# Attention and gated MLP on one core: loads of batch 1 taken ahead of w_out, transposes spread over the h steps, and k of batch 0 loaded as fp32 and cast on chip

## The chip, the cores and the metric

One NeuronCore of a Trainium2 chip runs the whole program. The metric is device time in microseconds (us) of one execution. PE is TensorE, the matmul engine; the profile calls GpSimd POOL, and SPq, ACTq and POOLq are the queues in which SyncE, ScalarE and GpSimd issue transfers. The granted clock is the share of its full clock that PE got, as the profile records it. An execution is called slow when it is over 1.5% above the fastest of the same kernel; ratios below use fast runs only.

## The reference

```python
# q, k, v: (8, 8, 576, 64) = batch, heads, sequence, head_dim; p: (8, 8, 32, 64)
p_packed = sm_attn(p, k, v)               # 32 rows attend to 576
out = sm_attn(q, p_packed, p_packed)      # 576 rows attend to the 32
x = out.transpose(0, 2, 1, 3).reshape(8 * 576, 512)
h = x @ w_in                              # 512 -> 2048
result = (h * cos(h)) @ w_out             # 2048 -> 512, fp32
```

`sm_attn` is softmax(scale · q kᵀ) v. All inputs are fp32 in HBM; the kernel works in bf16.

## The kernel before

The program is one hand-made schedule: instructions of an engine run in the order in which they are written. For each batch b there is an attention part that ends in `a2n[b]` (the normalised second softmax) and `PPW[b]` (the packed p times w_in), then an *h phase* of 16 steps. One step is four matmuls, a cosine on ScalarE (ACT) and a multiplication on VectorE (DVE) that writes `gT`. The output matmuls of batch b, gT times w_out, are *filler*: 64 or 80 matmuls of 0.2155 us that are slipped in wherever PE would otherwise wait during batch b+1. Batch 0 has no filler beside it. The k, q and v inputs are cast to bf16 in their transfers by GpSimd's queue; k and q are then transposed on PE in the first batches and by a DMA transpose on SyncE (`xbar`) later. In the code below `pe_T` transposes on PE, `s1` and `s2` are the scores and exponentials of the two softmaxes, `a1_pe` transposes the first one's result, `pp` multiplies it by v, `ppw` multiplies that by a quarter of w_in, `pack_p` transposes p, and `warm(n)` issues n matmuls on zeros that only keep PE busy.

```python
def load(n, b):                       # cast load, fp32 -> bf16, GpSimd's queue; one buffer for each of k, q, v
    bf[n, b] = bf_pool.tile([TP, H, C * D], BF16, name=n + "bf", tag=n + "bf")
    G.dma_start(out=bf[n, b], in_=srcs[n][b].rearrange("h (p c) d -> p h (c d)", c=C))

def xbar(n, b):                       # DMA transpose, SyncE's queue
    t = xT[n, b] = att_pool.tile([128, H * 3, TP], BF16, name=n + "T", tag=n + "T")
    nc.sync.dma_start_transpose(out=t, in_=bf[n, b].rearrange("p h x -> p (h x)"))
# ... (cut)
nc.sync.dma_start(out=p_raw[:, 0:2, :], in_=p_rows[:, 0:2, :])
load("k", 0); load("v", 0); make_identity(nc, ident); load("q", 0)
load_w_in(0); load_w_in(1)
G.dma_start(out=p_raw[:, 2:, :], in_=p_rows[:, 2:, :])
load_w_in(2); load_w_in(3)
for n in range(4): load_w_out(n)
load("k", 1); load("v", 1); load("q", 1); load("k", 2); load("v", 2); load("q", 2)
# ...
warm(7); dup_p(0, 2); pack_p(0, 1)    # p of batches 0 and 1: cast on DVE, transposes on PE
warm(9); pe_T("k", 0, (V, ACT, V)); s1(0); permute_v(0, V)
# ... attention of batch 0
for fc in range(NFC):                 # h phase of batch 0
    h_mm(0, fc)()
    if fc in (1, 4, 7): ppw(0, 1 + fc // 3)
    if fc == 10: pack_p(1, 3)
set_filler(0)
# ... attention of batch 1, with k2's transposes and s1(2) in it, 43 fillers
def begin_loads(b):                   # loads of batch 3 wait for the transpose of k3
    G.tensor_copy(out=gate, in_=xT["k", b][0:1, 0, 0:1])
    for n, i in (("v", b), ("q", b), ("k", b + 1)): load(n, i)
permute_v(2); xbar("q", 2); xbar("k", 3)     # DMA transposes BEFORE the h phase of batch 1
slot(1, [...], [(8, lambda: begin_loads(3)), (12, lambda: pw2(2))])
for s in range(2, B): ...             # batches 2 to 7
```

The softmax here doesn't subtract the row's maximum and nothing guards it: scores larger than these inputs give would overflow.

## Time and profile before

| | value |
|---|---|
| time, 3 runs | 263.75, 263.75, 261.2 us |
| span of the profiled run | 261.1 us, mean granted clock 0.993 |
| first h matmul of batch 0 | 20.27 us |
| last gT of batch 0 | 37.2 us |
| first h matmul of batch 1 | 58.27 us |
| last gT of batch 1 | 77.8 us |
| start of batch 3's second scores | 106.04 us |

The last five rows are landmarks from the timeline; they cut the program into stretches. The prediction shows the rows of the page and reads them. Two lines of the timeline of the kernel before: the cast of p (the number in brackets is DVE's wait for it) and the transposes of k of batch 0, which start when its cast load has landed.

```profile
2.89 0.40 DVE L303 CAST p_bf<-p_raw 128x128 bf16<-128x128 f32 x2 [0.64 <-DMA p_raw<-in_p_dram]
...
7.81 1.19 PE L101 MATMUL psA<-ident,kbf 96*128 96x96 bf16 x24 [0.88 <-DMA kbf<-in_k_dram]
```

### The profile page before, as it was taken

What the parts mean: (1) busy time and instruction counts of PE and PEld (TensorE: products, weight loads), DVE (VectorE), ACT (ScalarE), POOL (GpSimd) and SP (SyncE); (2) the same over time, 40 slices, a digit from 0 to 9 for tenths busy, and PEclk for the clock granted to TensorE, in tenths of its full rate; (3) what the DMA queues carried; (4) which work ended last, traced back from release to release, by engine and by line L of the source; (5) the groups of instructions that cost most, each with busy time, mean ns of one, the idle gap of its engine ahead of it and who ended that gap; (6) DMA issues with size and microseconds to landing.
All of it is one profiled execution on the core that took longest, in us unless ns stands there. A gap on an engine that the chain in (4) does not pass through costs nothing.

```text
span 261.1 us, 5031 instructions
## 1 busy us (share of the span) xinstructions
PE 236.6 (91%) x2004; PEld 133.3 (51%) x2037; DVE 165.6 (63%) x253; ACT 166.6 (64%) x270; POOL 53.6 (21%) x67
## 2 busy tenths in 40 slices
PE   8675759898989999999999999999989999999993
PEld 3443425644644565456545654465446564565452
DVE  2448864839875677658875676578846775687110
ACT  1378762297687766886788666877786576884000
POOL 8523002250404040504050304020310000000000
PEclk9999997999999999999999999999999999999999
DMA  6999999999499989599939994989294111111232
GB/s 90 203 227 208 206 204 179 180 177 197 77 191 209 198 134 231 108 191 164 220 81 191 171 219 103 158 179 173 77 139 109 40 43 40 40 46 47 69 83 80
DMA packets 62919, 37.09 MB, mean 142 GB/s; under 512 B 35520, under 2 KB 58304, under 8 KB 62896
## 3 DMA queue, kind: packets, MB, share of 16 engines
q0 software_dynamic: 23168, 18.81, 47.8%
q1 hardware_dynamic: 39568, 17.83, 32.7%
q8 instruction: 16, 0.26, 0.4%
q10 hardware_dynamic: 160, 0.13, 0.2%
q14 instruction: 7, 0.06, 0.1%
HBM read 37.22 MB, written 9.44 MB: 179 GB/s over the span
## 4 chain that ended last, share of the span: by engine, by line
PE 72%; DMA 13%; ACT 6%; DVE 4%; issue 2%; POOL 1%; DVEq 0%; POOLq 0%; ACTq 0%
PE ot L270 42%; PE psA L220 20%; DMA kbf<-in_k_dram 7%; DMA w_in_bf<-in_moe_w_in_dram 6%; PE psA L181 3%; PE psA L162 2%; DVE gT L227 2%; PE psA L101 1%; PE ot L259 1%; ACT cosT L224 1%; PE psA L197 1%; PE psA L123 1%; ACT a2u L189 1%; ACT L430 1%; ACT PPW L74 1%
## 5 line engine op out<-in xcount | busy, mean ns | idle before, releaser
L270 PE MATMUL ot<-w_out_bf,gT 128*128 128x512 bf16 x481 | 125.2, 381 | 1.7 <-issue 1.0
L227 DVE TENSOR_TENSOR gT<-psA,cosT 128x576 bf16<-128x576 f32 x128 | 93.8, 754 | 28.7 <-ACT cosT L224 27.2
L224 ACT ACTIVATE cosT<-psA 128x576 bf16<-128x576 f32 x128 | 81.5, 651 | 30.3 <-PE psA L220 28.2
L220 PE MATMUL psA<-a2n,PPW 128*128 128x288 bf16 x512 | 81.2, 285 | 7.4 <-DVE gT L227 3.6
L270 PEld LDWEIGHTS <-gT 128*128 128x128 bf16 x512 | 48.0, 98 | 44.9 <-issue 7.8
L220 PEld LDWEIGHTS <-PPW 128*128 128x128 bf16 x512 | 49.9, 97 | 39.9 <-issue 12.5
L76 DVE CAST PPW<-psA 128x1024 bf16<-128x1024 f32 x22 | 26.9, 1221 | 11.8 <-PE psA L181 11.8
L231 POOL COPY joint<-gT 128x512 bf16<-128x512 bf16 x16 | 9.7, 612 | 102.2 <-DVE gT L227 102.2
L76 DVE COPY osb<-ot 128x512 f32<-128x512 f32 (+1 forms) x19 | 12.8, 672 | 17.6 <-PE ot L270 14.1
L207 DVE SCALAR_TENSOR_TENSOR a2n<-a2u,r,lns 128x576 bf16<-128x576 bf16 x16 | 12.4, 814 | 16.0 <-ACT lns L205 16.0
L74 ACT COPY osb<-ot 128x512 f32<-128x512 f32 (+1 forms) x18 | 10.4, 575 | 17.9 <-PE ot L270 13.2
L76 POOL COPY vp<-vbf 96x3072 bf16<-96x3072 bf16 x6 | 16.5, 2747 | 0.6 <-DMA vbf<-in_v_dram 0.6
L132 ACT ACTIVATE a<-psA 128x576 bf16<-128x576 f32 x16 | 10.2, 648 | 8.3 <-PE psA L123 8.3
L199 ACT ACTIVATE lns<-psA 128x576 f32<-128x576 f32 x16 | 10.4, 653 | 5.7 <-PE psA L197 5.2
L74 ACT CAST PPW<-psA 128x1024 bf16<-128x1024 f32 x10 | 10.1, 1012 | 5.5 <-PE psA L181 5.5
L181 PE MATMUL psA<-w_in_bf,ppT 64*32 64x512 bf16 x256 | 11.9, 382 | 1.3 <-DVE gT L227 0.9
L189 ACT ACTIVATE a2u<-psA,rs 128x576 bf16<-128x576 f32 x16 | 11.0, 736 | 2.6 <-PE psA L123 2.4
L270 PE MATMUL ot<-w_out_bf,joint 128*128 128x512 bf16 x48 | 12.3, 379 | 0.2
L172 ACT CAST ppT<-psA 64x128 bf16<-64x128 f32 x16 | 4.2, 260 | 11.2 <-PE psA L101 6.4
L83 POOL DMA_DIRECT2D kbf<-in_k_dram x8 | 6.3, 786 | 22.1 <-PE psA L101 18.0
L444 POOL COPY gate<-a1T 1x1 bf16<-1x1 bf16 x5 | 0.9, 180 | 46.2 <-DMA a1T<-a 46.2
L224 ACT ACT_TABLE_LOAD x8 | 10.3, 1283 | 0.1
(54 smaller groups left out, 150.8 us busy)
## 6 DMA issues: line engine op xcount, KB each, us to landing
kbf<-in_k_dram POOLq DMA_DIRECT2D x8, 576.0 KB, 11.4
vbf<-in_v_dram POOLq DMA_DIRECT2D x8, 576.0 KB, 6.6
qbf<-in_q_dram POOLq DMA_DIRECT2D x8, 576.0 KB, 9.4
out_dram<-osb SPq DMA_DIRECT2D x24, 192.0 KB, 2.9
out_dram<-osb SPq DMA_DIRECT2D x22, 128.0 KB, 2.4
w_in_bf<-in_moe_w_in_dram POOLq DMA_DIRECT2D x4, 512.0 KB, 15.9
w_out_bf<-in_moe_w_out_dram POOLq DMA_DIRECT2D x4, 512.0 KB, 20.2
out_dram<-osb SPq DMA_DIRECT2D x26, 64.0 KB, 2.1
```

The source lines that it names most:

```text
L74: ACT.copy(out=out, in_=in_)
L76: eng.tensor_copy(out=out, in_=in_)
L132: ACT.activation(out=a1[b % 2][:, y, :, 0:TP].rearrange("p (e m) x -> p e m x", e=2), in_=ps[y][:, :, 0:HS].rearrange("p e (m x) -> p e m ...
L181: nc.tensor.matmul(ps[32 * x:32 * x + 32, y, :], ppT[b % 2][r, 2 * x + y, :], w_in_bf[r, x, n * 512:(n + 1) * 512], start=True, stop=True)
L189: ACT.activation(out=a2u[b][:, y].rearrange("p (e x) -> p e x", e=2), in_=ps[y][:, :, 0:HS], func=AF.Exp, scale=rs1[b][:, y:y + 1])
L199: ACT.activation(out=lns[b][:, y].rearrange("p (e x) -> p e x", e=2), in_=ps[:, :, 0:HS], func=AF.Ln)
L207: V.scalar_tensor_tensor(out=a2n[b][:, y], in0=a2u[b][:, y], scalar=r1[b][:, y:y + 1], in1=lns[b][:, y], op0=ALU.mult, op1=ALU.mult)
L220: nc.tensor.matmul(ps[:, e, 0:HS], PPW[b][:, y, fc * 128:(fc + 1) * 128], a2n[b][:, y, e * HS:(e + 1) * HS], start=(y == 0), stop=(y == 1))
L224: ACT.activation(out=csv, in_=ps[:, :, 0:HS], func=AF.Sin, bias=PI_HALF)
L227: V.tensor_tensor(out=gT[b][:, fc, :].rearrange("p (e x) -> p e x", e=2), in0=ps[:, :, 0:HS], in1=csv, op=ALU.mult)
L231: G.tensor_copy(out=joint[b // 2][:, fc - 7:fc + 1, j0:j0 + 64], in_=gT[b][:, fc - 7:fc + 1, 512:576])
L270: nc.tensor.matmul(ps, w, w_out_bf[:, fc, :], start=(fc == 0), stop=(fc == NFC - 1))
```

## The change

The intent has three parts. **Head:** k0 comes as plain fp32 in two halves by SyncE's queue and is cast by DVE and ACT, so the cast queue starts with v0; v0's permutation is split over DVE and GpSimd; p moves to ScalarE's queue. **Order of loads:** k1, v1 and q1 come ahead of w_out, so PE need not wait for k1 at 35 to 39 us. **Pacing:** k1 is transposed inside batch 0's h phase, k2 and q2 inside batch 1's, and filler is spread evenly. For this k gets two bf16 and two transposed buffers. The cut parts of the diff also compute the first two output chunks of batch 0 side by side, cast the rest of p on GpSimd instead of DVE and re-pace the filler of later batches.

```diff
-    nc.sync.dma_start(out=p_raw[:, 0:2, :], in_=p_rows[:, 0:2, :])
-    load("k", 0)
+    k0 = first.tile([TP, H, C * D], FP32, name="k0")
+    for hh in (slice(0, 4), slice(4, 8)):
+        nc.sync.dma_start(out=k0[:, hh], in_=k[0, hh].rearrange("h (p c) d -> p h (c d)", c=C))
+    nc.scalar.dma_start(out=p_raw[:, 0:2, :], in_=p_rows[:, 0:2, :])
     load("v", 0)
     make_identity(nc, ident)
     load("q", 0)
-    (w_in 0, 1, p, w_in 2, 3, w_out 0..3, k1, v1, q1, k2, v2, q2)
+    (w_in 0..3, p, k1; later in program order v1, q1, w_out 0..3, k2, v2)
 ... (cut)
-    pe_T("k", 0, (V, ACT, V))
+    for a in (0, 4):
+        copy(V, bf["k", 0][:, a:a + 3], k0[:, a:a + 3])
+        copy(ACT, bf["k", 0][:, a + 3:a + 4], k0[:, a + 3:a + 4])
+        if a == 0:
+            warm(2)
+            pe_T("k", 0, (V, ACT, V), (0,))
+            warm(5)
+    pe_T("k", 0, (V, ACT, V), (1, 2))
     s1(0)
-    permute_v(0, V)
+    permute_v(0, V, G)
 ... (cut; in batch 0's h phase:)
-            ppw(0, 1 + fc // 3)
+            ppw(0, 1 + fc // 3, ACT)
+        if fc == 12:
+            pe_T("k", 1)
 ... (cut; batch 1, and its h phase:)
-    permute_v(2); xbar("q", 2); xbar("k", 3)
-    slot(1, [...], [(8, lambda: begin_loads(3)), (12, lambda: pw2(2))])
+    slot(1, [(1, tk("k", 2, 0)), (2, tk("k", 2, 1)), (3, tk("k", 2, 2)), (4, lambda: ppw(1, 3, ACT)),
+             (6, lambda: pack_p(3, B)),
+             (8, tk("q", 2, 0)), (9, tk("q", 2, 1)), (10, tk("q", 2, 2)), (10, lambda: load("q", 3)),
+             (10, lambda: load("k", 4)), (11, lambda: xbar("k", 3))], 4)
 ... (cut: s1(2), attention of batch 2 and s1(3) now follow batch 1's h phase)
```

More of the change, by code (lines that the diff above doesn't have):

```diff
@@ L39 @@
     const = ctx.enter_context(tc.tile_pool(name="const", bufs=1))
+    first = ctx.enter_context(tc.tile_pool(name="first", bufs=1))
     bf_pool = ctx.enter_context(tc.tile_pool(name="bf", bufs=1))
@@ L81, in load, with permute_v, pe_T @@
     def load(n, b):
-        bf[n, b] = bf_pool.tile([TP, H, C * D], BF16, name=n + "bf", tag=n + "bf")
+        bf[n, b] = bf_pool.tile([TP, H, C * D], BF16, name=n + "bf", tag=n + "bf", bufs=2 if n == "k" else 1)
         G.dma_start(out=bf[n, b], in_=srcs[n][b].rearrange("h (p c) d -> p h (c d)", c=C))
-    def permute_v(b, eng=G):
+    def permute_v(b, eng=G, split=None):
         vp[b] = vp_pool.tile([TP, C, H * D], BF16, name="vp", tag="vp")
-        copy(eng, vp[b].rearrange("p c (h d) -> p c h d", h=H),
-             bf["v", b].rearrange("p h (c d) -> p c h d", c=C))
+        dst = vp[b].rearrange("p c (h d) -> p c h d", h=H)
+        src = bf["v", b].rearrange("p h (c d) -> p c h d", c=C)
+        if split is None:
+            copy(eng, dst, src)
+        else:
+            copy(eng, dst[:, :, 0:4], src[:, :, 0:4])
+            copy(split, dst[:, :, 4:8], src[:, :, 4:8])
     def xbar(n, b):
-        t = xT[n, b] = att_pool.tile([128, H * 3, TP], BF16, name=n + "T", tag=n + "T")
+        t = xT[n, b] = att_pool.tile([128, H * 3, TP], BF16, name=n + "T", tag=n + "T", bufs=2 if n == "k" else 1)
         nc.sync.dma_start_transpose(out=t, in_=bf[n, b].rearrange("p h x -> p (h x)"))
-    def pe_T(n, b, engs=(V, V, V)):
-        t = xT[n, b] = att_pool.tile([128, H * 3, TP], BF16, name=n + "T", tag=n + "T")
+    def pe_T(n, b, engs=(V, V, V), groups=(0, 1, 2)):
+        if 0 in groups:
+            xT[n, b] = att_pool.tile([128, H * 3, TP], BF16, name=n + "T", tag=n + "T", bufs=2 if n == "k" else 1)
+        t = xT[n, b]
         flat = bf[n, b].rearrange("p h x -> p (h x)")
-        for i in range(3):
+        for i in groups:
             ps = psa(BF16)
@@ L147, in a1_xbar, with a1_pe @@
                                     in_=a1[b % 2].rearrange("p a c x -> p (a c x)"))
-    def a1_pe(b):
-        t = a1T[b] = att_pool.tile([128, 2, C, 128], BF16, name="a1T", tag="a1T")
-        for y in range(2):
+    def a1_pe(b, ys=(0, 1)):
+        if 0 in ys:
+            a1T[b] = att_pool.tile([128, 2, C, 128], BF16, name="a1T", tag="a1T")
+        t = a1T[b]
+        for y in ys:
             ps = psa(BF16)
@@ L265, in out_gen @@
     def out_gen(b):
-        for c in range(n_chunks(b)):
-            ps = O.tile([128, DM], FP32, name="ot", tag="ot")
-            for fc in range(NFC):
-                w = joint[b // 2][:, fc, :] if c == 4 else gT[b][:, fc, c * 128:(c + 1) * 128]
-                nc.tensor.matmul(ps, w, w_out_bf[:, fc, :], start=(fc == 0), stop=(fc == NFC - 1))
-                if fc < NFC - 1:
-                    yield
-            osb = o_pool.tile([128, DM], FP32, name="osb")
-            copy((V, ACT)[n_out[0] % 2], osb, ps)
-            n_out[0] += 1
-            for a, z, rows in pieces_of(b, c):
-                nc.sync.dma_start(out=rows, in_=osb[a:z, :])
-            yield
+        groups = [(0, 1), (2,), (3,)] if b == 0 else [(c,) for c in range(n_chunks(b))]
+        for grp in groups:
+            pss = {c: O.tile([128, DM], FP32, name="ot", tag="ot") for c in grp}
+            for f0 in range(0, NFC, 4):
+                for c in grp:
+                    for fc in range(f0, f0 + 4):
+                        w = joint[b // 2][:, fc, :] if c == 4 else gT[b][:, fc, c * 128:(c + 1) * 128]
+                        nc.tensor.matmul(pss[c], w, w_out_bf[:, fc, :],
+                                         start=(fc == 0), stop=(fc == NFC - 1))
+                        if fc == NFC - 1:
+                            osb = o_pool.tile([128, DM], FP32, name="osb")
+                            copy((V, ACT)[n_out[0] % 2], osb, pss[c])
+                            n_out[0] += 1
+                            for a, z, rows in pieces_of(b, c):
+                                nc.sync.dma_start(out=rows, in_=osb[a:z, :])
+                        yield
     filler = [None, 0]
@@ L299, in load_w_out, with dup_p @@
                     in_=moe_w_out.rearrange("(a p) n -> p a n", p=128)[:, n * 4:(n + 1) * 4, :])
-    def dup_p(a, b):
+    def dup_p(a, b, eng):
         for t in range(2):
-            V.tensor_copy(out=p_bf[:, a:b, t, :], in_=p_raw[:, a:b, :])
+            eng.tensor_copy(out=p_bf[:, a:b, t, :], in_=p_raw[:, a:b, :])
     def warm(n):
@@ L307, in warm @@
             nc.tensor.matmul(wps, wz[:, 0:128], wz, start=True, stop=True)
-    nc.sync.dma_start(out=p_raw[:, 0:2, :], in_=p_rows[:, 0:2, :])
-    load("k", 0)
+    k0 = first.tile([TP, H, C * D], FP32, name="k0")
+    for hh in (slice(0, 4), slice(4, 8)):
+        nc.sync.dma_start(out=k0[:, hh], in_=k[0, hh].rearrange("h (p c) d -> p h (c d)", c=C))
+    nc.scalar.dma_start(out=p_raw[:, 0:2, :], in_=p_rows[:, 0:2, :])
+    bf["k", 0] = bf_pool.tile([TP, H, C * D], BF16, name="kbf", tag="kbf", bufs=2)
     load("v", 0)
@@ L313 @@
     load("q", 0)
-    load_w_in(0)
-    load_w_in(1)
+    for n in range(4):
+        load_w_in(n)
     G.dma_start(out=p_raw[:, 2:, :], in_=p_rows[:, 2:, :])
-    load_w_in(2)
-    load_w_in(3)
-    for n in range(4):
-        load_w_out(n)
     load("k", 1)
-    load("v", 1)
-    load("q", 1)
-    load("k", 2)
-    load("v", 2)
-    load("q", 2)
     wz = const.tile([128, 512], BF16, name="wz")
@@ L337 @@
     warm(7)
-    dup_p(0, 2)
+    dup_p(0, 2, V)
     pack_p(0, 1)
-    warm(9)
-    pe_T("k", 0, (V, ACT, V))
+    for a in (0, 4):
[6 more added lines that the diff above has]
+    pe_T("k", 0, (V, ACT, V), (1, 2))
     s1(0)
-    permute_v(0, V)
+    permute_v(0, V, G)
+    load("v", 1)
     warm(3)
@@ L348 @@
     pe_T("q", 0, (V, ACT, V))
+    load("q", 1)
+    for n in range(4):
+        load_w_out(n)
+    dup_p(2, 16, G)
+    load("k", 2)
+    permute_v(1, G)
+    load("v", 2)
     s2(0)
@@ L354 @@
     warm(6)
-    dup_p(2, 16)
     for fc in range(NFC):
@@ L358, with slot, pw2, tk @@
         if fc in (1, 4, 7):
-            ppw(0, 1 + fc // 3)
+            ppw(0, 1 + fc // 3, ACT)
         if fc == 10:
             pack_p(1, 3)
+        if fc == 12:
+            pe_T("k", 1)
+    def slot(s, hooks, keep=0, heavy={}):
+        left = filler[1] - keep
+        weight = [1 + heavy.get(fc, 0) for fc in range(NFC)]
+        for fc in range(NFC):
+            h_mm(s, fc)()
+            quota = (left * sum(weight[:fc + 1])) // sum(weight) - (left + keep - filler[1])
+            first = quota
+            while hooks and hooks[0][0] == fc:
+                if first == quota and fc in heavy:
+                    first = quota // 2
+                    fill(first)
+                hooks.pop(0)[1]()
+            fill(quota - first if first != quota else quota)
+    def pw2(b, n=0):
+        ppw(b, n)
+        ppw(b, n + 1)
+    def tk(n, b, i):
+        return lambda: pe_T(n, b, (V, V, V), (i,))
     set_filler(0)
     ACT.preload_act_table_set(EXP_SET)
-    fill(4)
-    pe_T("k", 1)
-    fill(3)
-    s1(1)
-    permute_v(1, V)
-    fill(8)
-    a1_pe(1)
-    recips(1)
-    fill(4)
+    s1(1)
+    pe_T("q", 1)
+    load("q", 2)
+    load("k", 3)
+    fill(5)
+    a1_pe(1, (0,))
+    fill(2)
+    a1_pe(1, (1,))
+    recips(1)
+    fill(3)
     pp(1)
-    pe_T("q", 1)
-    fill(3)
-    ppw(1, 0)
+    fill(6)
     s2(1)
-    fill(4)
-    pe_T("k", 2)
-    ppw(1, 1)
-    fill(3)
-    s1(2)
+    ppw(1, 0, V)
     fill(4)
     sums2(1, 0)
-    fill(4)
     sums2(1, 1)
@@ L389 @@
     fill(6)
-    a1_pe(2)
-    recips(2)
-    load("k", 3)
-    def slot(s, pieces, hooks, keep=5):
-        left = filler[1] - keep
-        for fc in range(NFC):
-            rest = h_mm(s, fc)
-            while pieces and pieces[0][0] == fc:
-                pieces.pop(0)[1]()
-            rest()
-            while hooks and hooks[0][0] == fc:
-                hooks.pop(0)[1]()
-            done = left + keep - filler[1]
-            fill((left * (fc + 1)) // NFC - done)
-    def pw(b, n):
-        return lambda: ppw(b, n)
-    def pw2(b):
-        fill(4)
-        ppw(b, 0)
-        ppw(b, 1)
-        fill(4)
-    def begin_loads(b):
-        G.tensor_copy(out=gate, in_=xT["k", b][0:1, 0, 0:1])
-        for n, i in (("v", b), ("q", b), ("k", b + 1)):
-            load(n, i)
-    permute_v(2)
-    xbar("q", 2)
-    xbar("k", 3)
-    slot(1, [(1, pw(1, 2)), (4, pw(1, 3)), (7, lambda: pp(2)), (9, lambda: pack_p(3, B)),
-             ], [(8, lambda: begin_loads(3)), (12, lambda: pw2(2))])
-    for s in range(2, B):
+    ppw(1, 1, V)
+    ppw(1, 2, V)
+    fill(4)
+    permute_v(2)
+    load("v", 3)
+    slot(1, [(1, tk("k", 2, 0)), (2, tk("k", 2, 1)), (3, tk("k", 2, 2)), (4, lambda: ppw(1, 3, ACT)),
+             (6, lambda: pack_p(3, B)),
+             (8, tk("q", 2, 0)), (9, tk("q", 2, 1)), (10, tk("q", 2, 2)), (10, lambda: load("q", 3)),
+             (10, lambda: load("k", 4)), (11, lambda: xbar("k", 3))], 4)
+    fill(1000)
+    set_filler(1)
+    ACT.preload_act_table_set(EXP_SET)
+    s1(2)
+    fill(9)
+    a1_pe(2, (0,))
+    fill(3)
+    a1_pe(2, (1,))
+    recips(2)
+    permute_v(3)
+    fill(3)
+    s1(3)
+    pp(2)
+    fill(6)
+    s2(2)
+    ppw(2, 0, V)
+    fill(8)
+    sums2(2, 0)
+    sums2(2, 1)
+    xbar("q", 3)
+    xbar("k", 4)
+    a1_xbar(3)
+    recips(3)
+    G.tensor_copy(out=gate, in_=a1T[3][0:1, 0, 0, 0:1])
+    normalise(2)
+    fill(8)
+    ppw(2, 1, V)
+    ppw(2, 2, V)
+    fill(8)
+    for n, b in (("v", 4), ("q", 4), ("k", 5)):
+        load(n, b)
+    slot(2, [(3, lambda: ppw(2, 3, ACT)), (7, lambda: pp(3)), (11, lambda: pw2(3))], 5, {11: 3})
+    for s in range(3, B):
         nxt = s + 1 < B
@@ L455 @@
                 load(n, b)
-        pieces = [(5, lambda: pp(s + 1))] if nxt else []
-        slot(s, pieces, [(9, lambda: pw2(s + 1))] if nxt else [])
+        slot(s, [(5, lambda: pp(s + 1)), (10, lambda: pw2(s + 1))] if nxt else [], 5, {10: 3})
     set_filler(B - 1)
```

## The prediction

> **What bounds the kernel now.** I read the page of the profile first: shares, slices, chain. The span is 261.1 us and PE is busy for 91% of it, so a change can win only where PE is idle, slow, or paced by another engine.
>
> ```profile
> PE 236.6 (91%) x2004; PEld 133.3 (51%) x2037; DVE 165.6 (63%) x253; ACT 166.6 (64%) x270; POOL 53.6 (21%) x67
> PE   8675759898989999999999999999989999999993
> PEclk9999997999999999999999999999999999999999
> DMA  6999999999499989599939994989294111111232
> ```
>
> One digit is 6.5 us. PE is below 9 only in the first seven slices; the DMA row is full there, and the one cold digit of the clock is slice 7 (39 to 46 us). Next, the chain of waits in order of time: its two longest pieces are transfers.
>
> ```profile
> 4.99 14.87 DMA w_in_bf<-in_moe_w_in_dram
> 20.42 18.85 DMA kbf<-in_k_dram
> 39.32 2.05 PE psA L101 x24
> ```
>
> k of batch 1 is issued at 20.4 us and lands at 39.3. Then I asked for each engine's busy time in stretches (engines from left to right, then clock, DMA, GB/s):
>
> ```profile
> 0.00:35.50 35.50, 25.84 (x245) 14.82 (x248) 21.67 (x43) 20.39 (x33) 12.96 (x21) 1.00 1.14 188
> 35.50:39.30 3.80, 1.03 (x5) 0.33 (x4) 1.60 (x3) 2.18 (x3) 0.00 (x0) 1.00 1.31 204
> 39.30:58.30 19.00, 17.88 (x225) 10.91 (x229) 10.29 (x20) 8.80 (x19) 6.99 (x7) 0.91 1.20 177
> 76.50:106.00 29.50, 28.45 (x232) 15.65 (x235) 20.34 (x29) 21.98 (x36) 6.46 (x8) 1.00 1.08 188
> 106.00:238.00 132.00, 128.30 (x1052) 71.98 (x1071) 91.67 (x130) 97.90 (x158) 23.60 (x26) 1.00 0.68 124
> ```
>
> From 76.5 us on PE is 97% busy. Idle or slow PE lies before: 3.8 us of waiting for k1, then a slow clock (0.72 in 40 to 45 us). In the timeline, PE from 20 to 35.5 us runs at DVE's pace:
>
> ```profile
> 39.31 1.84 PEld L101 LDWEIGHTS <-kbf 96*128 96x128 bf16 x24 [3.22 <-DMA kbf<-in_k_dram]
> 33.60 3.60 DVE L227 TENSOR_TENSOR gT<-psA,cosT 128x576 bf16<-128x576 f32 x5 [0.43 <-ACT cosT L224]
> 21.35 1.16 DVE L303 CAST p_bf<-p_raw 128x896 bf16<-128x896 f32 x2 [0.41 <-DMA p_raw<-in_p_dram]
> 10.67 0.95 DVE L76 COPY vp<-vbf 96x3072 bf16<-96x3072 bf16 x1 [1.08 <-DMA vbf<-in_v_dram]
> ```
>
> **What the Trainium skill says.** (1) "DMA: Bandwidth & Descriptors", Issuing engines are not separate DMA queues: transfers of all issuing engines share the same 16 DMA engines. The trace agrees in that the cast loads move 204 to 207 GB/s of bf16 from 7 to 35 us whatever is queued; so order decides when a tensor lands, and another queue only fills time in which the engines were idle. (2) Same page, SWDGE vs HWDGE vs iDMA: a cast in the transfer is possible on GpSimd's queue only. This is why k0 needs fp32 space and casts on chip; no run yet shows their cost. (3) "TensorE: Matmul & The Clock Gate", Part 1: after a window of some 3.4 us with an idle array the clock halves. Here PE worked 1.03 us of 3.8, and afterwards 24 transposes took 2.05 us instead of 1.19 (k0), so it agrees. (4) "GPSIMD Engine Reference", 3.1: elementwise work is slower on GpSimd. Agrees: the v permutation takes 2747 ns there, 955 on DVE.
>
> **The change, part by part.**
>
> *Head (0 to first h matmul, 20.27 before).* k0 leaves the cast queue. Before, it landed at 7.8 us, while the DMA engines moved only 17 to 57 GB/s until 4 us. p_raw by SyncE took 2.1 us from issue to landing. At an estimated 400 GB/s (twice the bf16 rate, fp32 read) each half of 590 KB takes 1.5 us: estimated landings 4.2 and 6.3. A cast of 1152 columns at the rate of the 896-column row (622 ns) is 0.8 us; DVE's copy of the first transposes (0.56) stands before the second cast, so that ends at about 7.7, the last kT copy at 9.4, and the first exp begins near 9.7 (9.98 before): 0.3 won, since the casts give back most of the earlier landing. v0 lands near 8.5 instead of 10.6 and half its permutation goes to GpSimd, so DVE no longer does 0.95 us of it at 10.67, just ahead of the a1T copies: 0.3 more. The rest of the chain (pp, q transposes, s2, sums, normalise) is the same. First h matmul at about 19.7: **0.6 us**.
>
> *First h phase (16 cos/mult steps; last gT at 37.2 before).* DVE bounds it: 16 x 0.754 = 12.1. It loses one PPW cast (1.22, to ACT) and the cast of p (1.16, to GpSimd, partly in a gap anyway), and gains three kT copies for batch 1 (3 x 0.555 = 1.67). ACT has 16 x 0.651 + 3 x 1.01 = 13.4, below. The phase keeps its length, about 15 us; last gT near 36.5, and k1 is then already transposed.
>
> *DMA order.* Per core the queue now is v0, q0, four w_in, p, k1, v1, q1, four w_out, k2. At 1.18 MB (fp32) a tensor, 1.05 a weight piece and about 0.4 MB/us, from q0 near 11.4: w_in to 22, k1 26, v1 29, q1 32, w_out 34, 37, 40, 42. k1 is needed near 31, and w_out by the output matmuls at about 36, 40, 43 and 45 (two chunks side by side, four contraction steps at a time, slow down the demand). All estimated; two us late would cost little.
>
> *Batch 1's attention (39.3 to first h matmul 58.27 before, 19.0).* Gone are the wait and the cold clock, and k2's transposes and s1(2), a1(2) move later. PE sum after: 30 fillers x 0.2155 = 6.5, q1's transposes 1.1, a1 0.8, pp 0.86, scores 0.7, sums 0.5, three ppw 1.0: 11.5. The chain beside it, from exp near 37 (table load 1.28 after the last cos), is exp 1.7, a1T 1.0, pp 0.9, ppT 1.1, s2 and exp 1.9, Ln and Exp 2.5, a2n 0.8, plus fillers that sit in between: first h matmul near 48.6, **9.7 us** earlier than before.
>
> *Second h phase.* This gives back. It takes k2's and q2's transposes (six DVE copies, 3.3) and 30 instead of about 16 fillers. From its first a2n DVE has 1.55 + two PPW 2.44 + 16 gT 11.8 + 3.3 + P copy 0.8 + two output copies 1.4 = 21.3, with gaps 22.5; before, from a2n at 57.40 to the last gT at 77.8, it was 20.4. So a2n 47.8, last gT 70.3: **7.5** remain.
>
> *Batch 2 to the start of batch 3's s2 (106.04 before).* After 70.3 PE has: fillers 80 x 0.2155 = 17.2, h 7.84, s1(2), a1(2), s1(3), pp(2), pp(3), s2, sums and six ppw 5.7: 30.7, and is the bound; before, s1(2), a1(2) and two ppw lay earlier and the stretch took 28.2. So batch 3 starts near 101.3: **4.7 us** remain.
>
> *Later batches.* Same work, PE 97% busy; the fillers around the two ppw are spread more evenly. Before, three h steps ran with no filler after them and PE waited 0.55 us for gT at 128.3. I give this 0.3 us in all.
>
> Sum: 4.7 + 0.3 = 5.0 us of 261.1.
>
> **Rivals.** (a) *The wait moves from k1 to w_out.* Total bytes are unchanged and the queue is full until 42 us, so w_out is last now. Should the last pieces land after 46, PE stalls in batch 1's attention, possibly long enough for a cold clock: gain 1 to 2.5 us, time about 261. For: the DMA row is full. Against: the demand is spread over 10 us, and the engines are busy 2.5 us earlier. (b) *DVE stays the bound of both early h phases and PE work is only moved.* The h phases hold 12 us of gT each; if copies and PSUM buffers (three) make the second phase 2 us longer than 22.5, gain 2.5 to 3, time about 260.5. For: before, DVE was busy 16.1 of 18.2 us there. (c) *More is won.* If the halves of k0 land a us sooner and the head's casts hide, and the even pacing keeps PE full in batches 1 and 2 (PE sum from first h phase to batch 3, 60 us, is the floor), batch 3 starts at 98 to 99: gain 7 to 8, time about 255.5. (d) *It is hidden anyway*: no; k1's landing is on the chain, with nothing else for PE to do.
>
> **Range and chances.** The runs before are 263.75, 263.75 and 261.2, the profiled one 262.84; taking off 5 gives 258.0, my prediction. Rivals (a) and (b) give the upper end, 261.3; (c) the lower, 254.6. A gain over 2% needs 5.3 us of 262.9, just above my central value: 0.45 for faster, 0.53 for within 2%, 0.02 for slower.
>
> **What would show it.** Right: no wait of PE for k of batch 1; clock 1.0 in all early slices; first h matmul at 19 to 20.5; batch 1's first h matmul at 47 to 50; last gT of batch 1 at 69 to 72; batch 3's s2 at 100 to 103; from there 155 us as before. A long wait of PE for w_out or q would prove rival (a); DVE over 90% busy in 48 to 70 with later landmarks, (b). It is wrong if k0's halves land after 8 us, if GpSimd's casts delay its own transfers, or if the gain sits after batch 3.

## The result, and the profile after

The changed kernel takes **272.31 us** (median of 4 runs, 271.34 to 273.58) against 262.48 for the kernel before (4 runs, 261.19 to 263.75): slower, ratio 1.0378, 95% interval 1.0294 to 1.0462. A ratio is the mean time of one kernel's fast runs over the mean of the other's fast runs of the same rounds, so it is not quite the ratio of the medians. The profiled span is 270.8 us.

First the page. The busy time of PE is not compared: the trace of before lacks some matmul records (481 of the 512 of gT times w_out are in it), so its sum is some us too low.

```profile
PE 245.3 (91%) x2059; PEld 135.7 (50%) x2059; DVE 165.4 (61%) x255; ACT 168.4 (62%) x272; POOL 58.5 (22%) x69
PE   4976778989994999999999999999999999999994
PEclk9999997999996899999999999999999999999999
DMA  6999999991298599969997998599666021111232
```

One digit is 6.8 us. PE has two new weak slices, the first (4 where before had 8) and the thirteenth (81 to 88 us, 4). The clock row has a cold digit at 41 to 47 us and two at 81 to 95. The DMA row falls to 1 and 2 at 61 to 74 us and is full again afterwards: transfers that used to be spread are bunched.

The stretches between the landmarks, in the order PE, PEld, DVE, ACT, POOL, then clock, DMA share and GB/s:

```profile
0.00:23.60 23.60, 16.60 (x153) 8.46 (x154) 10.14 (x27) 9.76 (x18) 12.64 (x20) 1.00 1.09 202
23.60:41.70 18.10, 13.09 (x132) 8.44 (x132) 13.61 (x21) 14.47 (x21) 7.42 (x7) 1.00 1.28 204
41.70:55.00 13.30, 12.77 (x134) 6.91 (x134) 5.99 (x12) 6.43 (x14) 5.57 (x5) 0.87 1.29 201
...
76.50:115.80 39.30, 34.27 (x312) 17.90 (x312) 21.91 (x35) 24.47 (x42) 6.39 (x7) 0.91 0.95 154
```

With the landmarks this gives the account. Each cell is a length in us; the last column comes from the best version that the experiments found.

| stretch | before | predicted | after | after less predicted | e9 (below) |
|---|---|---|---|---|---|
| start to first h matmul | 20.3 | 19.7 | 23.6 | +3.9 | 20.1 |
| batch 0's h phase, to the last gT | 16.9 | 16.8 | 18.1 | +1.3 | 18.1 |
| to batch 1's first h matmul | 21.1 | 12.1 | 13.3 | +1.2 | 11.7 |
| batch 1's h phase, to the last gT | 19.6 | 21.7 | 21.8 | +0.1 | 21.8 |
| to batch 3's second scores | 28.2 | 31.0 | 39.0 | +8.0 | 32.6 |
| batch 3's second scores begin at | 106.0 | 101.3 | 115.8 | +14.5 | 104.3 |

From there both kernels need 155.0 us. The wait for k1 is gone and batch 1's attention is 7.7 us shorter, as intended. What was lost lies in two places.

**The head.** Lines of the timeline, with each wait in brackets:

```profile
6.00 0.59 DVE L316 CAST p_bf<-p_raw 128x128 bf16<-128x128 f32 x2 [3.76 <-DMA p_raw<-in_p_dram]
...
8.50 0.51 ACT L75 CAST kbf<-k 96x384 bf16<-96x384 f32 x1 [1.67 <-DMA k<-in_k_dram]
8.84 2.33 PE L320 MATMUL wps<-wz 128*128 128x512 bf16 x5
...
23.61 0.41 PE L230 MATMUL psA<-a2n,PPW 128*128 128x288 bf16 x2 [0.87 <-DVE a2n L217]
```

p, 64 KB, lands at 5.98 us instead of 2.85. DVE takes its instructions in order, so it stands for 3.76 us, and PE waits 2.29 us for it. PE's five warming matmuls at 8.84 us then take 0.47 us each, where matmuls of this shape take 0.216 later on. But PE was no faster ahead of the wait: the first seven warming matmuls took 0.45 us each (3.17 us in all, as in the kernel before, where the next nine, without such a wait, took 2.56). The second half of k0 lands only at 8.50, later than the whole bf16 k0 landed before (7.81), and its casts come on top.

**The stretch to batch 3.** The chain of waits in order of time now has a DMA transpose in it that the chain of before had not:

```profile
0.74 5.24 DMA p_raw<-in_p_dram
...
72.09 13.26 DMA kT<-kbf
85.39 0.68 PE psA L131 x16
```

The timeline shows what was issued just ahead of it:

```profile
70.95 0.77 POOL L84 DMA_DIRECT2D qbf<-in_q_dram  x1 [2.37 <-PE psA L109]
71.71 0.77 POOL L84 DMA_DIRECT2D kbf<-in_k_dram  x1
72.09 7.61 SPq L98 DMA_TRANSPOSE kT<-kbf  x1
...
85.39 0.68 PE L131 MATMUL psA<-kT,P 64*32 64x288 bf16 x16 [3.92 <-DMA kT<-kbf]
```

k3's transpose takes 13.3 us, PE waits 3.9 us for it at 81.5 to 85.4, and the clock record then reads half speed. Before, this transpose stood ahead of batch 1's h phase in the program, with the loads gated behind it, and it landed in 4.7 us:

```profile
62.04 2.90 SPq L92 DMA_TRANSPOSE kT<-kbf  x1
```

### The profile page after: what moved, and what is told of

Its sections match the earlier page's. It is cut to its first block, busy times and chain, and to the rows that moved or that the text cites. A ratio compares the mean times of both kernels' runs of the same rounds, so it can differ in the third digit from the quotient of the medians.

```text
span 270.8 us, 5110 instructions
## 1 busy us (share of the span) xinstructions
PE 245.3 (91%) x2059; PEld 135.7 (50%) x2059; DVE 165.4 (61%) x255; ACT 168.4 (62%) x272; POOL 58.5 (22%) x69
## 4 chain that ended last, share of the span: by engine, by line
PE 66%; DVE 12%; ACT 11%; DMA 7%; issue 2%; ACTq 0%; DVEq 0%
PE ot L283 37%; PE psA L230 17%; DVE gT L237 6%; DMA kT<-kbf 5%; ACT cosT L234 4%; PE psA L191 3%; DMA p_raw<-in_p_dram 2%; PE psA L172 2%; PE psA L131 2%; PE psA L109 2%; DVE a2n L217 2%; DVE PPW L77 2%; ACT a2u L199 2%; ACT lns L209 1%; PE ot L269 1%
## 5 line engine op out<-in xcount | busy, mean ns | idle before, releaser
L283 PE MATMUL ot<-w_out_bf,gT 128*128 128x512 bf16 x512 | 135.7, 385 | 0.0
L230 PE MATMUL psA<-a2n,PPW 128*128 128x288 bf16 x512 | 83.0, 285 | 5.5 <-DVE gT L237 3.5
L230 PEld LDWEIGHTS <-PPW 128*128 128x128 bf16 x512 | 49.9, 97 | 40.2 <-issue 10.9
L77 DVE COPY osb<-ot 128x512 f32<-128x512 f32 (+1 forms) x19 | 12.8, 672 | 16.9 <-PE ot L283 13.8
L77 POOL COPY vp<-vbf 96x3072 bf16<-96x3072 bf16 (+1 forms) x8 | 20.7, 2586 | 10.4 <-DMA vbf<-in_v_dram 10.4
L283 PE MATMUL ot<-w_out_bf,joint 128*128 128x512 bf16 x48 | 13.0, 379 | 0.0
L215 ACT ACTIVATE lns<-lns 128x576 f32<-128x576 f32 x16 | 10.0, 680 | 0.0
L320 PE MATMUL wps<-wz 128*128 128x512 bf16 x23 | 8.8, 533 | 1.2 <-DVE wz L336 1.2
```

The source lines that it names most:

```text
L77: eng.tensor_copy(out=out, in_=in_)
L215: ACT.activation(out=lns[b][:, y], in_=lns[b][:, y], func=AF.Exp, scale=-1.0)
L230: nc.tensor.matmul(ps[:, e, 0:HS], PPW[b][:, y, fc * 128:(fc + 1) * 128], a2n[b][:, y, e * HS:(e + 1) * HS], start=(y == 0), stop=(y == 1))
L283: nc.tensor.matmul(pss[c], w, w_out_bf[:, fc, :], start=(fc == 0), stop=(fc == NFC - 1))
```

## The experiments

Two theories of the loss were stated: the head (with a rival about which of its parts costs) and the collision of k3's transpose with cast loads (with the rival that the transpose is merely issued late). All kernels gave correct results. The kernel before had medians of 262.5 to 262.6 us. Diffs are against the changed kernel unless said otherwise.

### 1 and 2: p first, and the two queues exchanged

```diff
 # e1_p_first
+    nc.sync.dma_start(out=p_raw[:, 0:2, :], in_=p_rows[:, 0:2, :])   # ahead of k0's halves
-    nc.scalar.dma_start(out=p_raw[:, 0:2, :], in_=p_rows[:, 0:2, :])
 # e2_swap
-        nc.sync.dma_start(out=k0[:, hh], ...)
+        nc.scalar.dma_start(out=k0[:, hh], ...)
-    nc.scalar.dma_start(out=p_raw[:, 0:2, :], ...)
+    nc.sync.dma_start(out=p_raw[:, 0:2, :], ...)
```

> Changed kernel, with the first 64 KB of p issued by SyncE ahead of k0's two halves instead of by ScalarE beside them. Theory: the head lost time because p (landing 5.98 us in the changed kernel, 2.85 before) shared the DMA engines with k0; DVE and PE waited for it in order, PE stood still for 2.3 us and then ran at half clock. Then p lands near 3, k0's halves stay near 6.3 and 8.5, PE keeps its clock, the first h matmul comes at 21 to 21.5 us instead of 23.6, and the kernel gains 2 to 2.5 us on the changed one (about 269). Rival: the fp32 load of k0 and its casts are the cost; then p lands early but the first h matmul stays near 23 and the time within 0.7 us of the changed kernel's.

> Changed kernel with the two queues swapped: p by SyncE, k0's halves by ScalarE. Theory (sharing of the DMA engines): p still lands at 5 to 6 us, on whichever queue it is. Rival (ScalarE's queue is slow to start or slow by itself): p lands near 3 us as it did by SyncE in the kernel before, and k0 lands later than 8.5.

e1: 273.0 us (272.88 to 274.9), ratio 1.0398 (1.0346 to 1.045): no gain over the change itself. e2, one look: 274.59 us. The DMA issues of e1, then of e2 (KB each, median us to landing):

```profile
p_raw<-in_p_dram SPq DMA_DIRECT2D x1, 64.0 KB, 2.0
k<-in_k_dram SPq DMA_DIRECT2D x2, 576.0 KB, 7.0
```

```profile
p_raw<-in_p_dram SPq DMA_DIRECT2D x1, 64.0 KB, 5.3
```

In e1 p lands in 2.0 us again, but k0's second half now only at 10.7, and the first h matmul comes at 24.38 instead of 23.61. So p's lateness was not what set the end of the head: that theory missed and the rival, k0's load, held. (The test is not clean: with p ahead of it k0's second half came 2.2 us later than in the changed kernel, and PE ran at a clock of 0.50 from 13 to 15 us.) In e2 p is slow on SyncE's queue as well (5.3 us), so ScalarE's queue was not the cause. p is slow when it shares the engines with k0 on another queue, and quick when it stands ahead of k0 in the same queue.

### 3: the loads behind the transpose

```diff
 # e3_gate
-             ... (10, lambda: load("q", 3)), (10, lambda: load("k", 4)), (11, lambda: xbar("k", 3))], 4)
+             ... (11, lambda: xbar("k", 3)),
+             (11, lambda: G.tensor_copy(out=gate, in_=xT["k", 3][0:1, 0, 0:1])),
+             (11, lambda: load("q", 3)), (11, lambda: load("k", 4))], 4)
```

> Changed kernel, with q3's and k4's loads moved behind k3's transpose and held until it has landed; the transpose is issued where it was. Theory: the transpose took 13.3 us to land because these two loads, issued 1.1 and 0.4 us ahead of it, share its DMA engines. Then it lands 5 to 6 us after its issue at 72 us, near 77.5, PE does not wait for it at 81.5 and keeps its clock, and the kernel gains 5 to 6.5 us (about 266). Rival 1: the transpose is slow for another reason (its place in SyncE's queue, the second buffer of k): it still lands after 83 and the time does not move. Rival 2: the loads, now later, bring a new wait for q3 or k4 and half of the gain is lost.

267.09, 263.45 and 266.12 us, and one slow run of 268.38; ratio 1.0098 (1.0019 to 1.0176). The timeline line of the transpose, issued 0.8 us *later* than in the changed kernel, and the landing times of tile kT in the window 60 to 100 us, first of the changed kernel, then of e3:

```profile
DMA to landing us min/median/max: 5.2/9.2/13.3
```

```profile
72.91 3.61 SPq L98 DMA_TRANSPOSE kT<-kbf  x1
...
DMA to landing us min/median/max: 5.0/5.2/5.4
```

The same transpose lands in at most 5.4 us instead of 13.3, PE no longer waits for kT, and from batch 2's first scores (77.32) to batch 3's second scores (110.33) there are 33.0 us instead of 39.3. The theory held: not the late issue but the two loads just ahead of it cost 6.3 us in this stretch.

### 4: the head of before in the changed order

```diff
 # e4_old_head: the fp32 k0, its casts and the split of v0 taken out
+    nc.sync.dma_start(out=p_raw[:, 0:2, :], in_=p_rows[:, 0:2, :])
+    load("k", 0)
 ...
+    warm(9)
+    pe_T("k", 0, (V, ACT, V))
-    permute_v(0, V, G)
+    permute_v(0, V)
```

> Changed kernel with the whole head of the kernel before (k0 cast by GpSimd's queue, p by SyncE, v0 permuted on DVE alone); everything after that as changed. Theory: the new head costs its 3.3 us in full and nothing of it is hidden later: first h matmul at 20.3, time about 3.3 us below the changed kernel's (about 269). Rival: later DMA waits (v1, w_out, k2 arrive by the queue's order, not by the head) take the gain back, and the time falls by less than 1.5 us.

267.77 us (267.43 to 268.21), ratio 1.0181 (1.0133 to 1.0229): 4.5 us below the changed kernel by the medians. The first h matmul is at 20.05 instead of 23.61, 3.56 us earlier. The wait of PE for the transpose stays:

```profile
PE psA L130 <- DMA kT<-kbf: 4.0, 1, 4.0
```

About one more us comes from the clock. After batch 0's h phase both kernels have a stretch in which PE is about half busy with the same work. In the changed kernel the clock falls in it, in e4 it does not. First two stretches of the changed kernel, then those of e4 with the same work, 3.5 us earlier (the clock is the third column from the right):

```profile
40.00:42.00 2.00, 0.92 (x23) 0.60 (x23) 1.66 (x3) 1.97 (x4) 0.28 (x1) 1.00 1.24 206
42.00:44.00 2.00, 1.48 (x23) 1.38 (x20) 1.07 (x2) 1.31 (x4) 0.34 (x1) 0.72 1.27 206
```

```profile
36.50:38.50 2.00, 0.98 (x24) 0.67 (x24) 1.59 (x3) 1.97 (x4) 0.67 (x2) 1.00 1.24 206
38.50:40.50 2.00, 1.43 (x23) 1.02 (x21) 1.36 (x3) 1.25 (x4) 0.47 (x2) 1.00 1.23 205
```

The same gap costs something in one kernel and nothing in the other; why is not shown by any run here.

### 5: is k0 slow by itself, or only beside the cast loads?

```diff
 # e5_hold: e1, and GpSimd's first load held until k0's second half has landed
     make_identity(nc, ident)
+    G.tensor_copy(out=gate, in_=k0[0:1, 4, 0:1])
     load("v", 0)
```

> As e1_p_first (p first on SyncE, then k0's fp32 halves), and GpSimd issues v0 and everything after it only when k0's second half has landed. Theory, after e1 and e2: k0's halves are late (6.3 and 10.7 us in e1) because the loads of GpSimd's queue, which stood behind k0 in the kernel before, now run beside it and take about half of the DMA engines. Then, alone, k0's second half lands by 6.5 us; v0 starts only then and lands near 11.5, so the first h matmul comes at 20 to 21.5 us and the time is 2 to 4 us under the changed kernel's (268.5 to 270). Rival: a load of k0 in fp32 is slow by itself (SyncE's path, rows of 1536 bytes, or the slow start of all DMA engines): the second half still lands after 8 us.

272.03, 272.86 and 273.42 us, and one slow run of 276.48, ratio 1.0452 (1.0386 to 1.0518). Alone on the engines the halves still land at 6.3 and 8.26 us. Two stretches of it: k0 alone, then cast loads alone (the last two columns are DMA share and GB/s written):

```profile
5.00:6.00 1.00, 0.05 (x1) 0.00 (x0) 0.00 (x0) 0.00 (x0) 0.00 (x0) 1.00 1.10 243
...
13.00:14.00 1.00, 0.54 (x6) 0.39 (x6) 0.00 (x0) 0.00 (x1) 1.00 (x2) 1.00 1.31 204
```

The DMA share is above 1 in both. The cast loads write 204 GB/s of bf16, so they read 408 GB/s of fp32; the plain fp32 load writes 241 to 269 GB/s and reads as much. k0 is 1.18 MB of fp32: at about 250 GB/s that is 4.7 us, against 2.9 us at the cast loads' rate. The rival held: the load is slow by itself. Which of its properties makes it slow is not shown. It is not SyncE's queue alone: on ScalarE's (e2) the casts of the halves begin at 6.34 and 8.75 us. Nor is it a ceiling on bytes written: in the kernel before the engines wrote 328 and 342 GB/s in the two half microseconds from 17.5 us, where the rest of p, a plain fp32 load by GpSimd, was the only queued load that does not cast (the prediction's 204 to 207 GB/s "whatever is queued" leaves this out). Holding the cast loads back made things worse, since v0 landed at 15.24 and the first h matmul came at 25.33.

### 6 and 7: both repairs, and the casts of PPW

```diff
 # e6_both: the edits of e3 and e4 together
 # e7_ppw: e6, and
-            ppw(0, 1 + fc // 3, ACT)
+            ppw(0, 1 + fc // 3)
```

> Changed kernel with both repairs: the head of the kernel before, and q3's and k4's loads held behind k3's transpose. Theory: the two losses are separate stretches of one serial schedule and add up; e4 gained 4.6 us on the changed kernel, e3 5.9; both give 10 to 11: 261.5 to 262.3, that is 0 to 1 us below the kernel before and not the 4 us below it that the prediction left for the rest of the change. Rival: once the head is early, another DMA wait appears or the two gains overlap, and it stays above 264.

> e6_both with the PPW casts of the first h phase on ScalarE, VectorE, ScalarE as in the kernel before, instead of ScalarE three times. In the changed kernel DVE waited 4.5 us for the cosines in that phase (1.9 in the kernel before), and the phase was 1.1 us longer than before although DVE had less to do. Theory: the step that bounds the phase is the round of three PSUM buffers through PE, ACT and DVE, and a cast put in front of the cosine lengthens it; then the phase gets 0.4 to 1 us shorter and the time falls by as much. Rival: the phase is bound by DVE's sum of work, as the prediction had it: then it gets 1.2 us longer.

e6: 261.38, 261.89, 261.38, 261.11, 261.41 us and one slow run of 266.7; ratio 0.9964 (0.9929 to 0.9999). Taken one at a time the two repairs won 4.5 and 6.2 us by the medians of the fast runs (e4, e3); together they win 10.9 (272.31 less 261.38), so the two gains add up, and they explain the whole loss. (e3's fast runs lie 3.6 us apart; by the profiled spans they are 4.6 and 5.5, and 11.2 with both.) What is left of the change is worth about 1 us over the kernel before, not the 5 that I predicted.

e7 asks why batch 0's h phase became 1.1 us longer: ACT got one more cast of PPW, and DVE waits for cosines in it 4.5 us in all, against 1.9 before. With the casts shared out again the times are 262.5, 262.61, 261.35, 261.37 and 261.8 us, and one slow 266.44, ratio 0.9983 (0.9945 to 1.002), half a us *more* than e6 by the means (261.93 against 261.43), which is within the noise. The gain of 0.4 to 1 us does not show, nor does the rival's loss of 1.2: both missed. (The phase is 19.5 us long in its profiled run, but with a cold clock at 22.5 to 26 us, so that length is no clean reading; the timed runs decide.)

### 8: the transpose early, the loads left as they were

```diff
 # e9_early: e4, and
-             (6, lambda: pack_p(3, B)),
+             (5, lambda: xbar("k", 3)), (6, lambda: pack_p(3, B)),
-             (10, lambda: load("k", 4)), (11, lambda: xbar("k", 3))], 4)
+             (10, lambda: load("k", 4))], 4)
```

> The head of the kernel before; q3's and k4's loads stay where the change has them, ungated, but k3's transpose is issued at step 5 instead of 11 of batch 1's h phase, in a stretch in which the DMA engines stand still. Theory: what cost the time is only that the transpose runs beside the two loads; out of their way it lands in 5 to 6 us and the time is that of e6_both within 1 us. Rival: SyncE's queue holds the transpose behind output stores whose data is not ready, so that moving it in the program does not move it in time, or it delays those stores and PE waits for output buffers: then the time stays 2 us or more above e6_both's.

**260.98 us** (260.86 to 261.18, 6 runs), ratio 0.9947 (0.9916 to 0.9978): the best version, 0.5% below the kernel before, and the steadiest. The transpose is issued at 56.96 us and has long landed when q3 and k4 are issued. The stretch to batch 3, and the page's clock row:

```profile
71.40:104.25 32.85, 31.37 (x301) 16.98 (x305) 21.85 (x35) 24.43 (x42) 6.39 (x7) 1.00 0.96 166
```

```profile
PEclk9999999999999999999999999999999999999999
```

PE is busy 31.4 of 32.9 us at full clock (its trace has 76 filler matmuls here where the changed kernel's has 81, so PE was busier still), so the stretch has nothing left to repair by waits; I had put its sum of PE work at 30.7 and the stretch at 31.

### 9 and 10: k1's transposes spread inside batch 0's h phase

```diff
 # e10_spread: e9, and
-        if fc == 12:
-            pe_T("k", 1)
+        if fc in (6, 9, 12):
+            pe_T("k", 1, groups=(fc // 3 - 2,))
 # e13_spread_late: e9, and the same with
+        if fc in (10, 12, 14):
+            pe_T("k", 1, groups=(fc // 2 - 5,))
```

> e9_early with the three groups of k1's transposes at steps 6, 9 and 12 of the first h phase instead of all at step 12. In e9 ACT waits 2.0 us at once for the next h tile while the three groups hold the three PSUM buffers; the phase was 1.1 us longer than predicted. Theory: it is this drain of the buffers that costs, not the three DVE copies; spread out, the phase gets 0.6 to 1.2 us shorter and the time falls by as much. Rival: the copies' DVE time (3 x 0.555 us) is the cost, and spreading changes nothing (within 0.3 us).

> As e10_spread, but k1's three groups of transposes at steps 10, 12 and 14, after k1 has landed (29.6 us in e10, where step 6 waited 2.8 us for it and PE fell to half clock, so that e10 told nothing of the buffers). Theory: the three groups at once hold all three PSUM buffers and drain the phase; spread, it gets 0.5 to 1.2 us shorter than in e9_early, and the time is 260 to 260.5. Rival: DVE's three copies are the cost, wherever they stand: within 0.3 us of e9_early (260.98).

The theory was that three groups of transposes in a row drain the three PSUM buffers. e10: 266.3 us (265.79 to 266.81), ratio 1.0147 (1.0113 to 1.0182), 5 us more than e9, but for another reason: k1 had not landed at step 6.

```profile
29.63 0.82 PE L108 MATMUL psA<-ident,kbf 96*128 96x96 bf16 x8 [2.83 <-DMA kbf<-in_k_dram]
```

```profile
30.00:35.00 5.00, 5.00 (x37) 2.92 (x35) 2.29 (x4) 2.91 (x4) 2.74 (x1) 0.50 1.29 205
```

One wait of 2.83 us is followed by five us at half clock. So e10 says nothing of buffers, but it prices an early wait. e13 moved the groups to where k1 is there: 262.28, 262.56 and 265.97 us and three slow runs of 266.26 to 267.04, ratio 1.0104 (1.0033 to 1.0175). In its profiled run the phase is 18.4 us long, against 18.1 in e9: not shorter. The theory of the drained buffers fell; the rival's forecast, within 0.3 us of e9, is not met either. Why the phase is 1.1 us longer than before stays open.

### 11 and 12: the new head alone, and the split of v0 alone

```diff
 # e11_head: the kernel BEFORE, and the fp32 k0 with its casts, p by ScalarE's queue; v0 permuted by DVE alone
 # e12_split: e9, and
-    permute_v(0, V)
+    permute_v(0, V, G)
```

> The kernel before with the new head alone (k0 in fp32 by SyncE and cast on chip into a buffer of its own, p by ScalarE, k0's transposes in two parts; v0 permuted by DVE alone, since its GpSimd half would stand behind loads that wait for it). Theory: the first h matmul is 3 to 3.6 us later, as in the changed kernel, but the kernel before waits for k1 until 39.3 anyway, so most of it is hidden: time within 1.2 us of the kernel before. Rival: the head's loss counts in full, 3 to 4 us slower, as e4 showed it in the changed order. (A loss above 4 us would be a loss of clock, which the page's clock row would show.)

> e9_early with v0's permutation split between DVE and GpSimd as the change has it (the only part of the new head that the prediction gave 0.3 us). Theory: DVE is free 0.4 us earlier for the a1T copies, but pp waits for GpSimd's half (1.46 us from v0's landing), so the first h matmul moves by less than 0.3 us and the time by less than 0.3 us. Rival: GpSimd's half delays its own queue of loads or pp, and the time grows by 0.5 us or more.

e11: 261.71 us (261.22 to 263.05), ratio 0.9981 (0.9937 to 1.0026): the same as before, although its first h matmul is 3.6 us later. Its lines of the timeline:

```profile
23.88 0.41 PE L228 MATMUL psA<-a2n,PPW 128*128 128x288 bf16 x2 [0.87 <-DVE a2n L215]
...
40.81 1.33 PE L109 MATMUL psA<-ident,kbf 96*128 96x96 bf16 x24
```

The second line has no bracket. With k1 still behind w_out in the queue, as before, it has landed by the time PE comes to it, and the late head costs nothing. Only when k1 was moved up did the head reach the critical path: the two parts of the change have to be judged together. e12: 261.46 us (260.94 to 262.75), ratio 0.9969 (0.9928 to 1.0009), first h matmul at 20.12 against 20.13: splitting v0's permutation wins nothing in the head. Its time is 0.5 us above e9's, which was taken on another chip; so the rival's loss of 0.5 us is neither shown nor excluded.

## Why the prediction was wrong, point by point

**Right.** No wait of PE for k1. Rival (a): no wait for w_out in the changed kernel, the rival did not occur. Batch 1's h phase: predicted 21.7 us, measured 21.8, so rival (b), an h phase well over 22.5 us, did not occur either. (That DVE sets this phase is not shown: of 21.5 us DVE was busy for 18.95 and PE for 19.8. And the other half of rival (b), that PE work is only moved, is largely what e9 shows below.) The later batches: predicted 0.3 us less, measured 155.0 against 155.1; pacing the filler more evenly won at most 0.1.

**Failed: the list of waits on the path of batch 2.** "After 70.3 PE has: fillers [...] and is the bound", 31 us. This sums PE's work and assumes that its inputs are there. I priced the loads of GpSimd's queue up to k2, none of batches 3 and 4, and no DMA transpose of SyncE's. The diff moves k3's transpose from ahead of batch 1's h phase to its step 11, takes away the gate of `begin_loads`, and with the second k buffer lets q3 and k4 load at step 10. All three could be read from it. Measured: 13.3 us to land, 3.9 us of waiting, half clock until about 90 us, 39.0 us in the stretch; with the loads behind it (e3), 6.3 us less. None of my rivals had this wait. Of the 8.0 us, some 6.4 are this (39.0 less e9's 32.6), the other 1.6 are PE work that I had put too low and a little idle time.

**Mis-sized: the rate of k0.** "At an estimated 400 GB/s (twice the bf16 rate, fp32 read)", halves at 4.2 and 6.3 us (the sum is off too: 1.5 us after 4.2 is 5.7). I took the rate at which cast loads *read* for the rate of a plain fp32 load. Measured 241 to 269 GB/s even alone (e5), halves at 6.3 and 8.5: the second half is 2.2 us late, after bf16 k0 would have landed. My own condition, "wrong if k0's halves land after 8 us", came true.

**Mis-sized: p.** I left p's 2.1 us out of the head's sum as if it kept it on the other queue. It took 5.24 us beside k0. e1 shows that repairing this alone wins nothing; what the waiting DVE and the still slow PE add to the head was not separated. Together the head came out at +3.3 us instead of −0.6, and e4 gives 4.5 us of time for it.

**Failed in batch 0's h phase, mis-sized elsewhere.** "DVE bounds it", "the phase keeps its length": 18.1 us instead of 16.9 before, in e9 too. DVE had less to do, 13.6 us in the phase, and waited 4.5 us for cosines (1.9 before), so it was not the bound. What is stays open: e7 and e13 speak against the PPW casts and the three groups of transposes in a row as simple causes. k1 landed at 29.5 us instead of 26, which cost nothing in the changed kernel (PE first needs it at 37); a like landing, 29.6, decided e10. And "clock 1.0 in all early slices": the clock fell to 0.50 at 44 to 46 us, and batch 1's attention took 13.3 us where e4's, at full clock, needed 11.7 (20.05 to the first h matmul, last gT at 38.1, batch 1's at 49.79).

**The gain that was hoped for.** With both losses repaired (e9) batch 3 begins at 104.3 us, 1.8 earlier than before, not the 4.7 predicted: the missing 3 us are 1.3 in batch 0's h phase, 1.6 in the stretch to batch 3, 0.4 in the head and 0.1 in batch 1's h phase, less 0.4 won in batch 1's attention. In e9 that attention is 9.4 us shorter than before, as the plan foresaw; nearly all of it is work that returns in the two later stretches (+2.2 and +4.4) and in batch 0's h phase (+1.2). Removing a wait of 3.8 us and a cold clock, with all that was moved for it, was worth 1.8.

## What to carry to other kernels

When a diff adds a buffer or moves a load, list every transfer that it lets start earlier and look what else is issued within a few us of it; a DMA transpose on the critical path belongs ahead of bulk loads, not behind them. Price a plain fp32 load by the rate of such a load (here about 250 GB/s), not by the read rate of cast loads, and a small transfer by whether it stands ahead of the bulk in its own queue. Before crediting the removal of a wait, subtract the work that used to fill it and must now be done elsewhere.

## What the Trainium skill lacked or had wrong

- "DMA: Bandwidth & Descriptors", Issuing engine by pattern, says that HWDGE (sync, scalar) is generally faster than GpSimd's queue. Here the fp32 k0 by SyncE landed at 8.26 us with the engines to itself (e5), the cast load of the same tensor by GpSimd at 7.8 with others queued behind it. The two do not write the same bytes, so "generally" may still hold. The page has no rates that compare a load that writes fp32 (241 to 269 GB/s written) with one that casts to bf16 (204 GB/s written, 408 read).
- Same page, Issuing engines are not separate DMA queues: agrees with e2 (p took 5.3 us on SyncE's queue too). The page has no number for what the sharing costs a small transfer: p, ahead of k0 in one queue, took 2.0 us (e1), and 5.2 when it got a queue of its own.
- Same page: what a DMA transpose costs beside ordinary loads is not given. Here 5.0 to 5.4 us when they were held behind it, 13.3 when two cast loads were issued just ahead.
- "TensorE: Matmul & The Clock Gate", Part 1, gives a window of about 3.4 us, running freely. Waits of PE shorter than that were followed by a granted clock of 0.50 here: 2.07 us in e5 (0.50 from 8 to 11 us), 2.73 us in the kernel before, at k1 (0.50 from 39.5 to 42.5 us), and 2.83 us in e10 (0.50 over five us). So the prediction's "so it agrees" goes too far: PE's own wait there was shorter than the window. In e7 the clock was 0.50 from 23 to 25 us though no single wait of PE in the eight us before was longer than 0.9 us. And a stretch with PE about half busy was followed by a slow clock in the changed kernel (0.72) and not in e4 (1.00). How short a wait is safe these runs do not answer; a window that runs freely would make it depend on where the wait lies, which no run here tested. The record of the clock itself is incomplete: the first seven warming matmuls took 0.45 us each while it read 1.00.
